# Entry to and exit from six seven-product steps: order lists, VectorE combinations and a further PSUM bank

## The chip, the cores and the metric

The kernel runs on one core of one Trainium2 chip. The metric is device time in microseconds (us) for one execution of the whole program. Three runs of the kernel before took 573.86, 575.05 and 577.16 us; the median is 575.05 us.

The engines are TensorE (PE in the rows; its weight loads are PEld), VectorE (DVE), ScalarE (ACT), GpSimd (POOL) and SyncE (SP, which here only issues DMAs). Each engine takes its instructions strictly in the order in which the program issues them.

## The reference

Attention with rotary embedding, then two feed-forward layers on its 1152 rows of 512 numbers (width inside: 2048). The change touches the first layer and the start of the second.

```python
x = attention(q, k, v)                    # (2, 8, 576, 64) -> (1152, 512)
h = x @ w_in                              # first layer, 512 -> 2048
g = np.where(h > 0, h, np.exp(np.minimum(h, 0)) - 1)
x = g @ w_out                             # 2048 -> 512
h = x @ w2_in                             # second layer
x = (h * np.tanh(np.log1p(np.exp(h)))) @ w2_out
```

## The kernel before, in words

Every matrix product is done as three products of rounded numbers: each operand is split into a high part (ScalarE rounds it) and a remainder (VectorE or GpSimd subtracts it), and high*high, high*low and low*high are added in PSUM. The weights come as 64-bit numbers (512 KB tiles `raw`, three buffers); ScalarE scales their high words (L96), VectorE puts the low bits in (L112, L123), ScalarE rounds (L128), and VectorE or GpSimd makes the remainder (L129).

The first layer has 16 blocks of 128 inner columns. Blocks 0 to 3 are done as six plain units, `units[0]` to `units[5]`: two blocks by a third (384) of the rows each, 24 pairs of matmuls in `g1_mm` (L211). Units 0 to 2 are multiplied in the tail of the attention. The units' way through the activation is `elu` (two ScalarE passes, L256 and L257), `elu_join` (VectorE, L261), `elu_hi` (ScalarE, L266) and `elu_lo` (VectorE, L270). Their product with `w_out` is twelve groups of 12 matmuls (`g2_mm`, L1012), three thirds by four slices; ScalarE copies each group out of PSUM into `Y` (L1041). These groups have two PSUM banks (`ps_h`), the units have two (`ps_s`).

Blocks 4 to 15 are done in pairs, six steps q = 2 to 7, each by a seven-product scheme in the manner of Strassen: `Pair.mm(1)` to `Pair.mm(7)`, here P1 to P7, 12 matmuls each at L1199, over combinations t1 to t4 of the inputs in each half of the rows (`form1`, L1090; their remainders `lo1`, L1094) and sums of the weights (`Pieces.sums`, L907). P1, P6, P7 and P4 add to one bank one after another, P5 and P3 to another, and ScalarE copies the state between them out (L1215); so P6 has to wait for the copy of P1, P7 for that of P6, P4 for that of P7. A step also runs the twelve groups of the step before (H0 to H11, six matmuls each, `g3_mm`, L1029); VectorE adds each into `Y` (L1043). P1, P5, P6 and P2 of a step come ahead of its H0. The order in a step is the hand-written list STEP, which `layer_step` plays.

Entry: `first` plays `unit_step(n)` for each unit, with the combinations of the inputs in between (`first_pieces`; t1 of both halves on GpSimd, the rest on VectorE), then STEP for q = 2, which runs the last four groups of the units when it comes to "or0". Exit: after STEP for q = 7, `seam` runs that step's own twelve groups, splits the new inputs (L1046, L1053) and forms the second layer's combinations (`form`, L975). `second` then does three plain units (`classic`, L211), three output groups (`out_mm`, L1426) and the second layer's steps, beginning with its P1.

The program is played in the order written (a manual schedule), so a list sets the order on all engines.

Of the kernel before, what the change touches and what calls it, by code (L numbers as in the profile page):

```python
# [26 lines left out]
def kernel(  # L27
# [23 lines left out]
    GF = 4  # L51
# [886 lines left out]
    def moe(mp, early):  # L938
# [96 lines left out]
        def g3_y():  # L1035
            if not sums1:
                return
            pair, t, e, o = sums1.pop(0)
            y = Yf[:, e, t * CH:t * CH + CH]
            if pair is None:  # L1040
                nc.scalar.activation(out=y, in_=o, func=AF.Copy)  # L1041
            else:
                nc.vector.tensor_tensor(out=y, in0=y, in1=o, op=ALU.add)  # L1043
            if pair is not None and pair.q == NF // 2 - 1 and e % 2:
                part = (slice(None), slice(e - 1, e + 1), slice(t * CH, t * CH + CH))
                nc.scalar.activation(out=XH[part], in_=Yf[part], func=AF.Copy)  # L1046
                late_xl.append((t, e, part))
            elif late_xl:
                last_xl()

        def last_xl():
            t, e, part = late_xl.pop(0)
            (nc.gpsimd if t and e == 1 else nc.vector).tensor_tensor(  # L1053
                out=XL[part], in0=Yf[part], in1=plain(XH[part]), op=ALU.subtract
            )

        pend, queue1, sums1, late_xl = [], [], [], []
# [38 lines left out]
        def unit_step(n):  # L1096
            m, fp, t = units[n]
            o = early.pop(n) if n in early else g1_mm(m, fp, t)

            def outs(k):  # L1100
                for _ in range(k):
                    if pend:
                        g3_mm()
                        g3_y()

            if n == 2:
                advance(0)
                advance(0)
                prefetch_weights(3)
            if o is not None:  # L1110
                o = elu(units[n], o)
                if n == 5:
                    put_hi(0, "t1")
                    put_hi(1, "t1")
                outs(1)
                o = elu_join(*o)
                if n == 5:
                    lo1(0, "t1", nc.vector)
                    lo1(1, "t1", nc.vector)
                o = elu_hi(*o)  # L1120
                outs(3)
                elu_lo(*o)
            first_pieces(n)
            if n % 2:
                pend.extend((t, e) for e in range(NC))

        ahead[:] = [3, 3]
        w2 = Pieces(0, GF // 2)

        def first_pieces(n):  # L1130
            D, G = nc.vector, nc.gpsimd
            if n == 2:
                w2.load(0)
                w2.load(1)
                for k in range(3):
                    form1(0, "t1", k, G)
                for k in range(3):
                    form1(0, "t3", k, D)
                w2.bits(0, 0, 1, 2)
                w2.bits(1, 0, 1, 2)  # L1140
                for k in range(3):
                    form1(1, "t1", k, G)
                for k in range(2):
# [36 lines left out]
        class Pair:  # L1180
# [96 lines left out]

        STEP = (
# [506 lines left out]
```

## Time and profile before

| what | value |
|---|---|
| runs, median (lowest, highest) | 575.05 us (573.86, 577.16) |
| the profiled execution: its own time | 575.36 us |
| its span in the trace | 573.2 us |
| mean granted TensorE clock | 0.97 of full |
| TensorE matmul busy | 544.3 us, 95% |
| VectorE, ScalarE, GpSimd busy | 436.8 (76%), 342.3 (60%), 221.1 us (39%) |

The time of the profiled execution is 2.2 us more than its span, for what lies around it. A share over the span mixes stages; a stage's own rows say what it waits for. The attention ends near 159 us, the six units and q = 2 lie between 159 and some 230 us, the even steps of 23.7 us run to about 328 us, the last step and the seam to 395 us, and the second layer to the end.

### The profile page before, as it was taken

The numbers are of one execution on the slowest core, as the hardware profiler recorded it, in microseconds if no ns is written. First come the engines' busy times: TensorE is split into PE (matmuls) and PEld (weight loads), VectorE is DVE, ScalarE is ACT, GpSimd is POOL, SyncE is SP. The second block draws the span as 40 slices with busy tenths as digits, with TensorE's granted clock in tenths as the row PEclk, the third lists the DMA queues.
The fourth block names the chain that finished last, engine by engine and source line by source line (L and its number), as shares of the span: only waits on it lengthen the run. The fifth ranks groups of instructions, "written<-read, shape, count | busy, mean of one in ns | idle before, by whom it ended". The sixth has DMA issues, their size and how long they took to land.

```text
span 573.2 us, 9332 instructions
## 1 busy us (share of the span) xinstructions
PE 544.3 (95%) x3436; PEld 490.8 (86%) x3436; DVE 436.8 (76%) x745; ACT 342.3 (60%) x640; POOL 221.1 (39%) x187
## 2 busy tenths in 40 slices
PE   8999999999997986899999996799999999999997
PEld 6778888888996885899999996798899888998986
DVE  6677777778778727878888787788788788878754
ACT  4766767777645426776666765357855546455430
POOL 7999989622293202232222321242012232123200
PEclk9999999999999878799999999699999999999999
DMA  6868889772312022314133142201331422313004
GB/s 207 215 187 223 225 211 245 174 184 86 112 37 75 0 74 73 113 35 148 38 111 112 37 148 74 73 1 38 110 114 40 141 74 74 120 39 100 1 1 165
DMA packets 49405, 60.70 MB, mean 106 GB/s; under 512 B 20944, under 2 KB 38736, under 8 KB 48592
## 3 DMA queue, kind: packets, MB, share of 16 engines
q1 hardware_dynamic: 48816, 59.52, 35.8%
q10 hardware_dynamic: 544, 0.59, 0.3%
q8 instruction: 27, 0.44, 0.3%
q14 instruction: 18, 0.15, 0.1%
HBM read 46.92 MB, written 2.36 MB: 86 GB/s over the span
## 4 chain that ended last, share of the span: by engine, by line
PE 78%; DVE 9%; ACT 4%; DMA 3%; issue 3%; SPq 2%; POOL 1%; ACTq 0%; POOLq 0%
PE ps_s L1199 25%; PE ps_h L1426 17%; PE ps_h L1029 12%; PE ps_s L479 6%; PE psA L599 5%; PE psT L559 4%; PE ps_s L211 3%; PE ps_h L1012 3%; DMA raw<-in_w_in_dram 2%; DVE ta L1090 1%; DMA v_t<-in_vp_dram 1%; SPq L380 1%; DVE gg L975 1%; DVE wv L112 1%; PE psA L668 1%
## 5 line engine op out<-in xcount | busy, mean ns | idle before, releaser
L491 DVE TENSOR_REDUCE mn<-ps_s 128x1 f32<-128x576 f32 x71 | 53.5, 757 | 24.1 <-PE ps_s L479 23.9
L1215 ACT ACTIVATE ta<-ps_s 128x576 f32<-128x576 f32 x58 | 37.5, 647 | 53.9 <-PE ps_s L1199 53.9
L1436 DVE TENSOR_TENSOR Y<-Y,ps_h 128x512 f32<-128x512 f32 (+1 forms) x64 | 43.4, 678 | 26.9 <-PE ps_h L1426 26.6
L513 ACT ACTIVATE P<-ps_s,mn 128x576 f32<-128x576 f32 x71 | 52.4, 739 | 10.6 <-DVE mn L491 9.4
L1043 DVE TENSOR_TENSOR Y<-Y,ps_h 128x384 f32<-128x384 f32 x72 | 39.1, 551 | 17.4 <-PE ps_h L1029 16.4
L1029 PE MATMUL ps_h<-gg,wo0bh 128*128 128x384 f32 x144 | 40.2, 362 | 6.6 <-ACT gg L1249 3.2
L1426 PE MATMUL ps_h<-wo0h,gg 128*128 128x512 f32 x144 | 45.3, 396 | 0.9 <-ACT Y L1434 0.9
L129 POOL TENSOR_TENSOR wo0l<-wu,wo0h 128x512 fp32r<-128x512 f32 x13 | 17.6, 1368 | 73.7 <-ACT wo0h L128 55.1
L1426 PE MATMUL ps_h<-wo0bh,gg 128*128 128x512 f32 (+2 forms) x148 | 45.7, 390 | 0.0
L559 PE MATMUL psT<-idn,P 128*128 128x128 f32 x288 | 42.9, 273 | 0.0
L129 POOL TENSOR_TENSOR wo0bl<-wu,wo0bh 128x512 fp32r<-128x512 f32 x12 | 15.9, 1340 | 64.1 <-ACT wo0bh L128 48.6
L579 ACT ACTIVATE pt<-psT 128x512 f32<-128x512 f32 x40 | 23.8, 594 | 25.7 <-PE psT L559 25.7
L1029 PE MATMUL ps_h<-gg,wo0h 128*128 128x384 f32 x144 | 36.9, 338 | 1.2 <-DVE Y L1043 1.2
L1252 DVE TENSOR_TENSOR gg<-ta,gg 128x576 fp32r<-128x576 f32 x46 | 35.7, 788 | 1.2 <-ACT gg L1249 0.8
L599 PE MATMUL psA<-pt,v_t 128*64 128x256 f32 (+1 forms) x240 | 35.9, 401 | 0.0
L559 PEld LDWEIGHTS psT<-idn,P 128*128 128x128 f32 x288 | 34.7, 141 | 1.3 <-ACT P L508 0.4
L1029 PEld LDWEIGHTS ps_h<-gg,wo0bh 128*128 128x128 f32 x144 | 27.8, 203 | 8.2 <-DVE Y L1043 4.0
L129 POOL TENSOR_TENSOR wi1l<-wv,wi1h 128x512 fp32r<-128x512 f32 x12 | 16.8, 1399 | 43.4 <-ACT wi1h L128 32.9
L1426 PEld LDWEIGHTS ps_h<-wo0bh,gg 128*128 128x128 f32 x148 | 26.9, 188 | 5.5 <-DVE Y L1436 0.2
L1426 PEld LDWEIGHTS ps_h<-wo0h,gg 128*128 128x128 f32 x144 | 26.1, 188 | 6.3 <-ACT Y L1434 1.3
L1249 ACT ACTIVATE gg<-ta 128x576 fp32r<-128x576 f32 x24 | 16.4, 684 | 24.9 <-DVE ta L1244 24.9
L129 POOL TENSOR_TENSOR wi0l<-wv,wi0h 128x512 fp32r<-128x512 f32 x14 | 19.6, 1400 | 24.8 <-ACT wi0h L128 21.1
(254 smaller groups left out, 1727.9 us busy)
## 6 DMA issues: line engine op xcount, KB each, us to landing
raw<-in_w_in_dram SPq DMA_DIRECT2D x32, 512.0 KB, 3.8
raw<-in_w_out_dram SPq DMA_DIRECT2D x32, 512.0 KB, 3.3
qk_t<-in_qk_dram SPq DMA_DIRECT2D x6, 1152.0 KB, 5.6
qa<-qh SPq DMA_DIRECT2D x28, 144.0 KB, 3.2
out_dram<-Y SPq DMA_DIRECT2D x8, 256.0 KB, 2.0
ka<-kh SPq DMA_DIRECT2D x14, 144.0 KB, 4.2
ka<-kl SPq DMA_DIRECT2D x14, 144.0 KB, 3.5
qb<-ql SPq DMA_DIRECT2D x14, 144.0 KB, 3.0
```

What stands on the lines that cost most here:

```text
L129: (by or nc.gpsimd).tensor_tensor(out=lo, in0=u, in1=plain(hi), op=ALU.subtract)
L491: nc.vector.tensor_reduce(out=m[:, 0:1], in_=psS[u][:, :, :HS], axis=AX.XY, op=ALU.min)
L513: nc.scalar.activation(out=P.rearrange("p (j n) -> p j n", j=2), in_=s[:, :, :HS], func=AF.Exp, scale=-1.0, bias=m, accum_out=sm_t[p, g][: ...
L559: nc.tensor.transpose(tv[:, c, :], P[:, k:k + 128], idn)
L599: nc.tensor.matmul(o[64 * h:64 * h + 64, cols], lhsT=v, rhs=rhs, start=(c == 0 and first), stop=(c == 4), skip_group_check=True,)
L1029: nc.tensor.matmul(o, lhsT=w[:, e * 128:e * 128 + 128], rhs=x, start=(k == 0), stop=(k == 5))
L1043: nc.vector.tensor_tensor(out=y, in0=y, in1=o, op=ALU.add)
L1199: nc.tensor.matmul(self.o[r][:, u, :H2], lhsT=w[i][:, cc, :], rhs=XO[u][xn][x][:, cc, :], start=(first and n == 0), stop=(last and n == 3 ...
L1215: nc.scalar.activation(out=self.temp(nm), in_=self.bank(r), func=AF.Copy)
L1252: (by or nc.vector).tensor_tensor(out=self.home(nm, 1), in0=self.temp(nm), in1=plain(self.home(nm, 0)), op=ALU.subtract)
L1426: nc.tensor.matmul(o, lhsT=l, rhs=w[:, es], start=(k == 0), stop=(k == 5))
L1436: nc.vector.tensor_tensor(out=y, in0=y, in1=o, op=ALU.add)
```

## The change: what it does

Three order lists take the place of `unit_step`, `first_pieces`, `seam` and the STEP of the first and the last step. BEGIN holds units 2 to 5 and step q = 2 in one list, LAST holds step q = 7 and the seam in one list; STEP stays for q = 3 to 6 (four entries that called nothing are gone from it). In the lists M is a unit's product, E, J, I, K its activation in the four parts above, H and Y a group and its eviction, f, h, l a combination, its rounding and its remainder, W, Q, S, R the weights of the first (in LAST: of the second layer's first) pair: scale, low bits, sums, rounding; small letters w, p, s, r the same for the next pair; o, or the output weights; c, d, e, x, h, l with m1, u2, u3 or s the activation of the four results of a step; C and D the rounding and remainder of the new inputs.

All combinations and their remainders in the entry are on VectorE. Unit 5 is multiplied into the bank that P5 and P3 use later (`spare_bank`), so units 3, 4 and 5 have three banks.

```diff
-        def unit_step(n):
-            m, fp, t = units[n]
-            o = early.pop(n) if n in early else g1_mm(m, fp, t)
...
-        def first_pieces(n):
-            D, G = nc.vector, nc.gpsimd
...
-                for k in range(3):
-                    form1(0, "t1", k, G)
...
-                for k in range(3):
-                    form1(1, "t1", k, G)
...
+        o2 = [Block(GF + j) for j in range(2)]
+
+        def spare_bank():
+            return g_pool[0].tile([128, 2, 512], F32, tag="s2", name="ps_s2", bufs=1)
...
+        BEGIN = (
+            "v", "W0", "f0t10", "E2", "W1", "J2", "H0", "Y0", "f0t30", "f0t31", "f0t32", "H1",
+            "f0t20", "Q10", "M3", "I2", "H2", "K2", "f0t11", "Y1", "Q00", "Q01", "f0t21", "Y2",
+            "M4", "f0t40", "E3", "f1t30", "f0t12", "H3", "Q11", "h0t1", "J3", "I3", "S3", "f0t41",
+            "M5", "K3", "h0t4", "S1", "l0t1", "S2", "E4", "S4", "J4", "R1", "R2", "I4",
+            "K4", "h0t3", "H4", "h0t2", "Y3", "l0t4", "R0", "E5", "R3", "Y4", "f1t31", "l0t3",
+            "P1", "J5", "f1t32", "h1t3", "f1t20", "I5", "f1t10", "f1t11", "f1t12", "H5", "H6", "Y5",
+            "A0", "h1t1", "A1", "f1t21", "P2", "l0t2", "w0", "l1t1", "Y6", "h1t2", "f1t40", "f1t41",
+            "p00", "K5", "h1t4", "l1t4", "H7", "cm1", "Y7", "l1t2", "dm1", "o00", "l1t3", "P5",
+            "p01", "cm5", "em1", "H8", "P6", "Y8", "o01", "xm1", "cu2", "P3", "du2", "P7",
+            "eu2", "xu2", "cu3", "d22", "hu2", "hm1", "eu3", "w1", "H9", "H10", "lu2", "Y9",
+            "o10", "lm1", "xu3", "P4", "hu3", "lu3", "p10", "p11", "Y10", "s3", "o11", "H11",
+            "r0", "s1", "or0", "cs", "Y11", "or1", "s2", "s4", "es", "r1", "a0", "r2",
+            "r3", "a1",
+        )
...
+        LAST = (
+            "P1", "w0", "cm1", "P5", "o00", "Xs", "o01", "cm5", "p00", "P6", "o10", "P3",
+            "Ks", "cu2", "o11", "or0", "Ls", "H0", "w1", "P2", "or1", "dm1", "P7", "p10",
+            "p11", "H1", "Y0", "p01", "Y1", "H2", "H3", "em1", "H4", "xm1", "r1", "Y2",
+            "du2", "Y3", "H5", "hm1", "a0", "lm1", "cu3", "eu2", "H6", "b0", "H7", "Y4",
+            "xu2", "r0", "P4", "H8", "Y5", "H9", "Y6", "hu2", "lu2", "d22", "Y7", "eu3",
+            "a1", "xu3", "Y8", "cs", "hu3", "H10", "Y9", "Y10", "es", "xs", "lu3", "W0",
+            "Q00", "W1", "H11", "Q01", "Y11", "hs", "Q10", "ls", "b1", "B0", "Q11", "q",
+            "H12", "mish", "H13", "Y12", "Y13", "B1", "S3", "C0", "H14", "S1", "H15", "H16",
+            "Y14", "Y15", "H17", "C1", "Y16", "H18", "D0", "S2", "Y17", "C2", "D2", "Y18",
+            "H19", "Y19", "R0", "S4", "H20", "H21", "D1", "H22", "C3", "Y20", "Y21", "Ft3",
+            "C4", "D3", "Y22", "Gt3", "H23", "Ft2", "Y23", "D4", "Ft4", "Gt2", "C5", "Lt2",
+            "Lt3", "D5",
+        )
...
+            dict(R0="DVE", R1="POOL", R2="DVE", R3="POOL", lm1="DVE", lu2="DVE", lu3="POOL", or0="DVE", or1="DVE", r0="DVE", r1="DVE", r2="DVE", r3="DVE"),
...
+            dict(B0="DVE", D0="POOL", D1="DVE", D2="DVE", D3="DVE", D4="DVE", D5="DVE", Ls="POOL", lm1="POOL", ls="DVE", lu2="POOL", lu3="POOL", or0="DVE", or1="DVE", r0="POOL", r1="DVE", r2="DVE", r3="POOL"),
...
+                elif k == "M":
+                    n = int(r)
+                    at[n] = g1_mm(*units[n], o=spare_bank() if n == 5 else None)
...
+                elif k == "f":
+                    form1(int(r[0]), r[1:3], int(r[3]), nc.vector)
...
+                elif k == "l":
+                    lo1(int(r[0]), r[1:], nc.vector)
...
-        def seam(x, o):
...
+                if q == GF // 2:
+                    layer_step(BEGIN, BY[0], x, None, w, o, on, w2)
...
+                    if q + 1 < NQ:
+                        layer_step(STEP, BY[1], x, prev, w, o, on)
+                    else:
+                        layer_step(LAST, BY[2], x, prev, w, o, on, ahead_pieces)
```

GpSimd in the entry, from the last output weights of the attention's tail to the first remainder of a result `gg`. The kernel before (L1090: t1; L1094: remainders of t2 to t4; L129: weights):

```order
L1090 TENSOR_TENSOR Y<-XH 128x2x288
L1090 TENSOR_TENSOR Y<-Y,XL 128x2x288 x2
L1090 TENSOR_TENSOR Y<-XH 128x2x288
L1090 TENSOR_TENSOR Y<-Y,XL 128x2x288 x2
L129 TENSOR_TENSOR wi1l<-wv,wi1h 128x512
L1094 TENSOR_TENSOR ge<-ta,ge 128x576 x2
L129 TENSOR_TENSOR wi1l<-ws,wi1h 128x512
L1094 TENSOR_TENSOR xt_2324<-ta,xt_2324 128x576
L129 TENSOR_TENSOR wo0l<-wu,wo0h 128x512
L1252 TENSOR_TENSOR gg<-ta,gg 128x2x288
```

The changed kernel, the same stretch of the same engine:

```order
L129 TENSOR_TENSOR wi1l<-wv,wi1h 128x512
L129 TENSOR_TENSOR wi1l<-ws,wi1h 128x256
L1169 TENSOR_TENSOR gg<-ta,gg 128x2x288
```

Six parts of t1 and three remainders have gone from GpSimd to VectorE, and two of the four weight remainders there have changed.

ScalarE in the entry, around the evictions of the second third of the units' groups (L1041). The kernel before; the first row is the high part of unit 3:

```order
L266 ACTIVATE gg<-tc 128x768
L998 ACTIVATE xt_2202<-ta 128x576
L128 ACTIVATE wi1h<-wv 128x512 x2
L998 ACTIVATE ge<-ta 128x576 x2
L256 ACTIVATE tc<-ps_s 128x768
L257 ACTIVATE tc<-tc 128x768
L1041 ACTIVATE Y<-ps_h 128x384
L266 ACTIVATE gg<-tc 128x768
L1041 ACTIVATE Y<-ps_h 128x384 x3
```

The changed kernel, from the fourth eviction (the last of the first third) on; `ps_s_2222` is unit 5 in the further bank:

```order
L1041 ACTIVATE Y<-ps_h 128x384
L128 ACTIVATE wi1h<-wv 128x512
L256 ACTIVATE tc<-ps_s_2222 128x768
L257 ACTIVATE tc<-tc 128x768
L128 ACTIVATE wi1h<-ws 128x256
L1041 ACTIVATE Y<-ps_h 128x384
L998 ACTIVATE xt_2316<-ta 128x576
L266 ACTIVATE gg<-tc 128x768
L1041 ACTIVATE Y<-ps_h 128x384
```

The evictions now stand one by one between the other work, and unit 5's activation comes ahead of the second third's evictions.

VectorE in the exit, around the remainder of the result s of step q = 7 (the remainders of results write `gg`; the join of s is the L1244 row, L1161 in the changed kernel). The kernel before, up to the first additions of that step's own groups:

```order
L112 TENSOR_SCALAR wu_3958<-wu_3958 128x512
L123 SCALAR_TENSOR_TENSOR wu_3958<-raw_3718,wu_3958 128x512
L1252 TENSOR_TENSOR gg_3853<-ta_3865,gg_3853 128x2x288
L1244 SCALAR_TENSOR_TENSOR ta_3949<-sa_3964,ta_3949 128x576
L1252 TENSOR_TENSOR gg_3853<-ta_3949,gg_3853 128x2x288
L112 TENSOR_SCALAR wv_3968<-wv_3968 128x512
L123 SCALAR_TENSOR_TENSOR wv_3968<-raw_3790,wv_3968 128x512
L112 TENSOR_SCALAR wv_3975<-wv_3975 128x512
L123 SCALAR_TENSOR_TENSOR wv_3975<-raw_3876,wv_3975 128x512
L1043 TENSOR_TENSOR Y_2053<-Y_2053,ps_h_3991 128x384
L1043 TENSOR_TENSOR Y_2053<-Y_2053,ps_h_3998 128x384
L1043 TENSOR_TENSOR Y_2053<-Y_2053,ps_h_4009 128x384
```

The changed kernel, from the join of s to the same additions:

```order
L1161 SCALAR_TENSOR_TENSOR ta_3942<-sa_3954,ta_3942 128x576
L112 TENSOR_SCALAR wv_3959<-wv_3959 128x512
L123 SCALAR_TENSOR_TENSOR wv_3959<-raw_3784,wv_3959 128x512
L1043 TENSOR_TENSOR Y_2053<-Y_2053,ps_h_3968 128x384
L112 TENSOR_SCALAR wv_3964<-wv_3964 128x512
L1169 TENSOR_TENSOR gg_3867<-ta_3942,gg_3867 128x2x288
L112 TENSOR_SCALAR wu_3936<-wu_3936 128x512
L123 SCALAR_TENSOR_TENSOR wu_3936<-raw_3718,wu_3936 128x512
L129 TENSOR_TENSOR wo0l_3983<-wu_3869,wo0h_3982 128x512
L123 SCALAR_TENSOR_TENSOR wv_3964<-raw_3871,wv_3964 128x512
L1043 TENSOR_TENSOR Y_2053<-Y_2053,ps_h_3987 128x384
L1043 TENSOR_TENSOR Y_2053<-Y_2053,ps_h_3997 128x384
```

The low bits of the second layer's output weights (`wu`), which stood ahead of the remainders of u3 and s, come behind that of s; the remainders of u2 and u3 have left the engine (they are on GpSimd), and the first layer's last addition and half of the next weights' low bits (`wv`) stand between the join of s and its remainder.

## Rows read from the trace of the kernel before

**Rows 1.** The page's line of the granted TensorE clock, 40 slices

```profile
PEclk9999999999999878799999999699999999999999
```

**Rows 2.** Windows: length, busy us (count) per engine, clock, DMA share, GB/s

```profile
158.90:239.80 80.90, 65.69 (x349) 62.55 (x349) 55.47 (x69) 43.10 (x73) 26.71 (x18) 0.85 0.17 54
242.05:265.77 23.72, 23.72 (x159) 23.72 (x158) 19.34 (x37) 15.59 (x27) 5.78 (x5) 1.00 0.28 79
328.46:395.40 66.94, 58.33 (x320) 55.23 (x320) 55.24 (x81) 37.20 (x58) 17.02 (x13) 0.92 0.20 63
198.20:208.40 10.20, 7.46 (x29) 7.11 (x30) 5.30 (x9) 2.90 (x5) 0.00 (x0) 0.50 0.33 102
358.60:368.70 10.10, 7.82 (x26) 7.32 (x25) 7.45 (x10) 3.31 (x5) 2.90 (x3) 0.50 0.33 104
```

**Rows 3.** The chain that ended last: start, length (us), work

```profile
189.86 4.20 PE ps_s L211 x24
...
209.15 8.49 PE ps_h L1012 x48
...
265.77 3.18 PE ps_s L1199 x24
268.95 6.24 PE ps_h L1029 x36
...
403.33 5.60 PE ps_h L1426 x24
```

**Rows 4.** Waits of TensorE, 158 to 240 us: total, times, longest

```profile
PE ps_s L1199 <- ACT ta L1215: 6.2, 3, 2.7
PE ps_s L1199 <- ACT wi0h L128: 3.9, 1, 3.9
PE ps_h L1012 <- ACT Y L1041: 3.1, 1, 3.1
```

**Rows 5.** Waits of TensorE, 328 to 396 us

```profile
PE ps_h L1029 <- DVE Y L1043: 4.1, 3, 2.3
PE ps_h L1029 <- ACT gg L1249: 3.2, 1, 3.2
```

**Rows 6.** Timeline of ScalarE, entry: start, length (us), instruction

```profile
182.56 0.84 ACT L257 ACTIVATE tc<-tc 128x768 f32<-128x768 f32 x1
183.31 0.47 ACT L1041 ACTIVATE Y<-ps_h 128x384 f32<-128x384 f32 x1
...
224.94 0.68 ACT L1239 ACTIVATE sa<-ta 128x576 f32<-128x576 f32 x1
225.66 0.68 ACT L1240 ACTIVATE sa<-sa 128x576 f32<-128x576 f32 x1
226.25 0.61 ACT L128 ACTIVATE wi0h<-wv 128x512 fp32r<-128x512 f32 x1
```

**Rows 7.** Timeline of VectorE, entry

```profile
164.12 1.98 DVE L1090 TENSOR_TENSOR ta<-XH 128x576 f32<-128x576 f32 x1
...
173.18 0.75 DVE L1090 TENSOR_TENSOR ta<-ta,XH 128x576 f32<-128x576 f32 x1
...
174.64 0.95 DVE L261 SCALAR_TENSOR_TENSOR tc<-tc,ps_s 128x768 f32<-128x768 f32 x1
...
203.30 0.42 DVE L112 TENSOR_SCALAR wv<-wv 128x512 int32<-128x512 int32 x1
203.64 0.68 DVE L123 SCALAR_TENSOR_TENSOR wu<-raw,wu 128x512 int32<-128x512 int32 x1
```

**Rows 8.** Timeline of GpSimd, entry

```profile
161.95 3.52 POOL L1090 TENSOR_TENSOR Y<-Y,XL 128x576 f32<-128x576 f32 x2
165.43 1.95 POOL L1090 TENSOR_TENSOR Y<-XH 128x576 f32<-128x576 f32 x1
```

**Rows 9.** The page's group of additions into Y: busy, mean ns

```profile
L1043 DVE TENSOR_TENSOR Y<-Y,ps_h 128x384 f32<-128x384 f32 x72 | 39.1, 551 | 17.4 <-PE ps_h L1029 16.4
```

**Rows 10.** Loads, 140 to 245 us: count, KB each, us to landing

```profile
raw<-in_w_in_dram SPq DMA_DIRECT2D x7, 512.0 KB, 3.8
```

More of the change, by code (lines that the diff above doesn't have):

```diff
@@ L1043, in g3_y @@
                 nc.vector.tensor_tensor(out=y, in0=y, in1=o, op=ALU.add)
[L1044 to L1057, printed above, removed]
+        pend, queue1, sums1 = [], [], []
         late_pool[0] = mp
@@ L1336, in layer_step @@
                 elif k == "o":
                     o[int(r[0])].bits(2 * int(r[1]))
-                elif k == "r":
-                    w.round(int(r), by(t))
+                elif k == "A":
+                    o[int(r)].load()
                 elif k == "a":
                     on[int(r)].load()
-                    if x.q == NF // 2 - 1:
-                        on[int(r)].bits(0, 1, 2)
+                elif k == "b":
+                    on[int(r)].bits(0, 1, 2)
+                elif k == "B":
+                    on[int(r)].round(eng(t))
+                elif k == "v":
+                    pend.extend((0, e) for e in range(NC))
+                    advance(0)
+                    advance(0)
+                    prefetch_weights(3)
+                elif k == "M":
+                    n = int(r)
+                    at[n] = g1_mm(*units[n], o=spare_bank() if n == 5 else None)
+                elif k == "E":
+                    at[int(r)] = elu(units[int(r)], at[int(r)])
+                elif k == "J":
+                    at[int(r)] = elu_join(*at[int(r)])
+                elif k == "I":
+                    at[int(r)] = elu_hi(*at[int(r)])
+                elif k == "K":
+                    n = int(r)
+                    elu_lo(*at[n])
+                    if n % 2:
+                        pend.extend((n // 2, e) for e in range(NC))
+                elif k == "f":
+                    form1(int(r[0]), r[1:3], int(r[3]), nc.vector)
+                elif k == "h":
+                    put_hi(int(r[0]), r[1:])
+                elif k == "l":
+                    lo1(int(r[0]), r[1:], nc.vector)
+                elif k == "q":
+                    queue1.extend((x, t, e) for t in range(NT // CH) for e in range(NC))
+                elif k == "C":
+                    nc.scalar.activation(out=XH[part(r)], in_=Yf[part(r)], func=AF.Copy)
+                elif k == "D":
+                    eng(t).tensor_tensor(out=XL[part(r)], in0=Yf[part(r)], in1=plain(XH[part(r)]), op=ALU.subtract)
+                elif t == "mish":
+                    warm = mp.tile([128, 1], F32, name="warm")
+                    nc.gpsimd.memset(warm, 0.0)
+                    nc.scalar.activation(out=warm, in_=warm, func=AF.Mish)
+                    mish[0] = True
+                elif k == "F":
+                    form(0, r)
+                elif k == "G":
+                    put_hi(0, r)
+                elif k == "L":
+                    put_lo(0, r)
+                else:
+                    raise ValueError(t)
@@ L1377, in first @@
                 o = on
             return x, o
-        def seam(x, o):
-            w = ahead_pieces
-            w.load(0)
-            x.join("s")
-            x.hi("s")
-            x.lo("s")
-            w.load(1)
-            w.bits(0, 0, 1, 2)
-            for b in o:
-                b.round()
-            w.bits(1, 0, 1, 2)
-            queue1.extend((x, t, e) for t in range(NT // CH) for e in range(NC))
-            for i in range(3 * NC):
-                g3_mm()
-                if i:
-                    g3_y()
-                if i == 1:
-                    warm = mp.tile([128, 1], F32, name="warm")
-                    nc.gpsimd.memset(warm, 0.0)
-                    nc.scalar.activation(out=warm, in_=warm, func=AF.Mish)
-                    mish[0] = True
-                if i in (3, 5):
-                    w.sums(*((0, 1) if i == 3 else (2, 3)))
-                if i == 10:
-                    form(0, "t3")
-                    w.round(0)
-                if i == 11:
-                    form(0, "t2")
-            g3_y()
-            last_xl()
-            form(0, "t4")
-            put_hi(0, "t3")
-            put_hi(0, "t2")
-            put_lo(0, "t3")
-            put_lo(0, "t2")
```

158 lines of the change are left out of this document (46 added, 112 removed), and 14 rows, old and new, of the table STEP.

## Prediction

> **What bounds the kernel now.** I read the page's clock line first, because a busy share of 95% hides where TensorE runs slowly: the slices that fall under full clock lie in two places, 186 to 244 us and 358 to 373 us [rows 1]. These are the entry to and the exit from the seven-product steps, the only places that the change touches. Then the windows [rows 2]. A step in the middle (242.05 to 265.77) keeps TensorE busy for all its 23.72 us at full clock, with VectorE busy 19.3 and ScalarE 15.6 us: such a step can't get shorter, and there is spare time beside it. The entry, from the end of unit 2 (158.9) to the first output group H0 of step q = 3 (239.8), takes 80.9 us with TensorE busy 65.7 at a mean clock of 0.85. The exit, from P1 of q = 7 (328.46) to the second layer's first P1 (395.4), takes 66.9 us with 58.3 busy at 0.92.
>
> Third, the waits of TensorE. In the entry [rows 4] it waits 6.2 us in three stays for ScalarE's copies between P1, P6, P7 and P4, because in STEP the last four groups' evictions stand in front of those copies; 3.9 us for the rounding of the next step's weights; and 3.1 us for an eviction into Y that stands behind both passes of unit 4's activation (it starts at 183.31, right after the pass from 182.56) [rows 6]. In the exit [rows 5] it waits 4.1 us for additions into Y and 3.2 us for the high part of the result s. The waits are paid again in clock: at 198.2 to 208.4 and 358.6 to 368.7, both behind waits, the granted clock was 0.50, that is the 1.2 GHz level, and TensorE was busy 7.5 and 7.8 us there [rows 2]. At full clock that work takes half, so each stretch cost 3.7 to 3.9 us.
>
> **What TensorE must do in any order.** Prices from the chain [rows 3]: a unit 4.20 us; a units' group 8.49 / 4 = 2.12; a product 3.18 / 2 = 1.59; a step's group 6.24 / 6 = 1.04; an output group 5.60 / 4 = 1.40. Entry: three units 12.6, twelve groups 25.5, seven products 11.1, then P1, P5, P6, P2 of q = 3 with 6.4: 55.6 us, so H0 of q = 3 can't come before 158.9 + 55.6 = 214.5. Exit: seven products 11.1, 24 groups 25.0, three units 12.6, three output groups 4.2: 52.9 of the 66.9 us. The most that the change can give is 25.3 + 14.0 = 39.3 us; no matmul is added or removed.
>
> **Entry, part by part.** The evictions stand singly and the four last groups are spread between the products, so each copy comes while a group runs: the 6.2 and 3.1 us have cover. Unit 5 in a further bank lets M5 run before unit 3's and unit 4's banks are read; its price is that P5 must wait until unit 5's join has read that bank, which stands 23 entries and several matmul groups ahead of P5: nothing.
>
> VectorE takes over nine instructions of the combinations from GpSimd, and four in all of q = 2's remainders. From the first part of t1 to the remainder of q = 2's s, which H0 of q = 3 needs, it has 78 instructions: 8 of 768 wide at 0.95 us, 38 of 576 wide at 0.75, 17 of 0.42 (9 shifts, 8 sums), 15 of 0.68 (7 low bits, 8 weight remainders, one of them half as wide) [rows 7]. That is 7.6 + 28.5 + 7.1 + 10.2 = 53.4 us; back to back each hides 0.08 of the one before (203.30 to 203.64 with 0.42), so 47.2 to 53.4 us from 158.9: ready between 206.1 and 212.3, under TensorE's 214.5 if it never waits. It is close, so every wait of VectorE counts in part.
>
> Such waits come from GpSimd: a combination of 0.75 us took 1.98 while GpSimd ran one, which itself took 1.95 against 3.52 / 2 = 1.76 [rows 7, 8]. So the two engines take turns. On GpSimd the six parts of t1 held VectorE off 1.76 us each, on VectorE they cost 0.75: 10.6 against 4.5 us, a gain. The changed entry keeps three instructions on GpSimd (R1, R3, and u3's remainder); each can hold VectorE up to 1.3. I take one such hold on the path, 1.3 us; bounds 0 and 3.9.
>
> Where the Trainium skill speaks against the change: Perfetto Trace Analysis, section Optimizing Scalar/DVE Operations, says that moving work between these two engines might not help, since they share a read port. By that rule the exchange gives nothing: the sum keeps its TensorE terms, and VectorE's 53.4 us, counted with the 6.1 that the exchange saves, come to 59.5 and over the floor by 3.9. The rows above show the sharing (1.98 against 0.75), and also that an instruction on VectorE takes its turn for less than half as long.
>
> What is late next is the hand-over to q = 3. After the last group H11, TensorE has P1 (1.59 us) and then P5, which needs r1, the last but two of the weight roundings. ScalarE has between H11 and r1 an eviction (0.47), a rounding (0.61), both passes of s (0.68 each) and r1 itself (0.61) [rows 6]: 3.05, less overlaps 2.7 to 3.0; P5 waits 1.1 to 1.5, I take 1.4. Behind r1 on ScalarE stands a0, the scaling of a weight tile whose buffer is freed by o11; a load lands in 3.8 us [rows 10], o11 comes some 4 us ahead of a0, so between 0 and 2 us for r2 and P6 behind it; I take 0, since it lies beside the wait for r1. VectorE's arrears of a few us are worked off in q = 3, which leaves it 4.4 us [rows 2].
>
> A wait of TensorE of about a microsecond may or may not bring the lower clock; I put in half of the price of one stretch, 1.9 us (bounds 0 and 3.9). Entry: 214.5 + 1.3 + 1.4 + 1.9 = 219.1 instead of 239.8: -20.7 us.
>
> **Exit, part by part.** VectorE has 81 instructions in 55.2 us there now [rows 2]; the lists move three result remainders and one input remainder to GpSimd and others back, so its work stays near that, under 52.9 only if GpSimd holds it off less than now (13 instructions then, as many now). The high part of s now comes behind a copy (0.61), two passes (1.37), the join (0.75) and two scalings, and its remainder (0.75) behind that: about 5 us after P4, against H8 to H11 (4.2): H12 waits 0.9 instead of 3.2. Behind that remainder VectorE has low bits, a weight remainder and low bits again (2.3 us) before the first addition (0.55 [rows 9]); H14 needs that addition's bank, 2.1 us after H12 starts: another 0.8. The input roundings and remainders come before their units need them; the second layer's combinations lie beside the three units. One hold by GpSimd 1.3 and half a slow stretch 1.9 as above: 52.9 + 0.9 + 0.8 + 1.3 + 1.9 = 57.8 instead of 66.9: -9.1 us.
>
> **Sum.** -20.7 - 9.1 = -29.8 us on the profiled execution's own time of 575.36 us: 545.6. That execution lies 0.3 us from the median of the runs, 575.05, so I take no difference and forecast 546. Two runs of this kernel differ by up to 0.6%, so about 0.5% is what can be told from no change.
>
> **Rivals.**
> - *VectorE becomes the bound.* For it: 53.4 us of work in a stretch whose floor is 55.6, with every activation join in the same queue. If it waits for others as much as in a full step (4.4 of 23.7 us), the entry is 53.4 + 3.9 + 55.6 x 4.4 / 23.7 = 67.6 us and, with TensorE waiting for it, two slow stretches, 7.7: 80.9 - 75.3 = 5.6 gained; the exit with two slow stretches is 63.6, 3.3 gained. Time 566; with only one of the two places so, 551 or 561. Against it: the lists put joins behind work that is ready.
> - *TensorE near its floor*: none of the added waits, 575.4 - 39.3 = 536 to 541. Against it: r1, which follows from the list.
> - *Not faster: the low clock stays.* If TensorE's small waits keep it at 1.2 GHz from unit 5 on, the work behind (eight groups, eleven products: 16.9 + 17.5 = 34.4 us) takes twice as long, +34.4, and undoes the whole entry's and exit's gain: about 575 to 580. It decides from some 30 us at the low level. Against it: in the full steps, where TensorE has work without end, the clock was 1.00, and in the lists it waits less than now, when two such stretches cost 10 us each. The Trainium skill, page TensorE: Matmul & The Clock Gate, section HAM oscillation, describes such loops that wait and go slow again each time; the trace agrees that it happens here, in two stretches of 10 us and no more.
> - *The change doesn't reach the bound*: loads set the time. Against it: no wait of TensorE in either place ends with a load [rows 4, 5]; 572 to 575.
>
> **How the numbers follow.** Forecast (its own range 541 to 552) 0.58; VectorE as the bound, in part or whole (552 to 566) 0.24; near the floor (536 to 541) 0.09; low clock 0.06; loads 0.03. The range 538 to 561 leaves out about 0.2: half of the floor case, the upper part of the second, and the last two. Faster by over 0.5%: 0.92; within 0.5%: 0.03; slower: 0.05.
>
> **What would show it.** Right: H0 of q = 3 near 219, the next full steps at 23.7 us, no six-microsecond wait for copies; P5 of q = 3 waiting for r1; the second layer's P1 some 58 us after P1 of q = 7; clock under 0.9 in no stretch over 10 us. Wrong: VectorE without idle time from 165 to 215 while TensorE waits for combinations or joins; several low stretches in the entry; a load as the releaser of a0 with P6 behind it.

## The result and the profile after

| | before | after |
|---|---|---|
| median of 4 runs | 574.83 us | 545.32 us (545.22 to 545.94) |
| ratio, 95% interval | | 0.9483 [0.9454, 0.9513] |
| profiled execution: time, span | 575.36, 573.2 us | 545.94, 544.1 us |
| mean granted clock | 0.97 | 0.997 |
| entry: unit 2's end to H0 of q = 3 | 80.9 us | 58.4 us |
| exit: P1 of q = 7 to the second layer's P1 | 66.9 us | 61.1 us |

The change is faster by 5.2%. The forecast was 546.0; of its two terms the entry came out 1.8 us better (-22.5 for -20.7) and the exit 3.3 us worse (-5.8 for -9.1), and the attention's end, which the forecast left where it was, came 0.8 us earlier. That the whole lies within 1 us of the forecast is in part luck: these errors cancel.

The page's clock line of the changed kernel, which answers to [rows 1]: one slice under full clock, in the exit, where before there were five.

```profile
PEclk9999999999999999999999998999999999999999
```

The windows of the changed kernel: entry (the row ends 0.16 us behind the first matmul of H0), a middle step, exit; then the exit's first half (seven products, H0 to H11), its twelve last groups (H12 to H23), in these the stretch behind the waits, and the exit's three units; last, VectorE's stretch from the join of s on. Columns as in [rows 2].

```profile
158.10:216.70 58.60, 56.51 (x351) 55.25 (x350) 52.21 (x81) 41.41 (x70) 5.67 (x5) 1.00 0.22 70
242.53:266.25 23.72, 23.72 (x159) 23.72 (x158) 19.19 (x35) 15.58 (x27) 5.25 (x6) 1.00 0.29 88
305.06:366.15 61.09, 56.98 (x320) 52.91 (x320) 51.68 (x81) 37.15 (x59) 17.32 (x12) 0.97 0.22 69
305.06:330.84 25.78, 24.66 (x157) 23.30 (x157) 19.84 (x34) 15.36 (x27) 7.48 (x6) 1.00 0.34 103
330.84:348.98 18.14, 15.35 (x74) 13.79 (x73) 15.29 (x29) 9.16 (x14) 4.82 (x3) 0.91 0.26 88
333.90:337.40 3.50, 3.50 (x11) 3.07 (x12) 3.29 (x7) 0.95 (x3) 1.49 (x1) 0.53 0.70 243
348.98:361.48 12.50, 12.50 (x73) 12.50 (x73) 12.32 (x15) 9.21 (x15) 5.02 (x3) 1.00 0.00 0
330.47:366.15 35.68, 32.69 (x167) 29.98 (x166) 32.21 (x49) 22.16 (x34) 9.93 (x8) 0.95 0.13 45
```

The middle step is what it was, 23.72 us, so all but the 0.8 us of the attention's end was won at the two ends. In the entry's row TensorE is busy 56.5 of 58.6 us at full clock. TensorE's waits in the entry of the changed kernel (total, times, longest), which answer to [rows 4]:

```profile
PE ps_s L1116 <- ACT ta L1132: 0.8, 1, 0.8
PE ps_s L1116 <- ACT wi0h L128: 0.7, 1, 0.7
PE ps_s L1116 <- DVE wi0l L129: 0.4, 1, 0.4
```

Of 6.2, 3.9 and 3.1 us are left 0.8 and 0.7, and 0.4 for a remainder on VectorE, all in the hand-over to q = 3. TensorE's waits in the exit, which answer to [rows 5]:

```profile
PE ps_h L1029 <- DVE Y L1043: 2.0, 4, 0.9
PE ps_h L1029 <- DVE gg L1169: 1.4, 1, 1.4
PE ps_h L1029 <- ACT gg L1166: 0.5, 1, 0.5
PE ps_h L1388 <- ACT Y L1396: 0.2, 1, 0.2
```

Group H12 waits twice for s, 0.5 us for its high part and 1.4 us for its remainder, and behind that TensorE runs at a granted clock of 0.53, the 1.2 GHz level, to 337.4. The other three executions had a mean clock of 1.000 and spans of 543.4 to 543.5 us: this stretch comes in some executions and costs 0.6 to 0.7 us.

### The profile page after: what moved, and what is told of

It reads as the page before. It is cut to its first block, busy times and chain, and to the rows that moved or that the text cites. A ratio compares the mean times of both kernels' runs of the same rounds, so it can differ in the third digit from the quotient of the medians.

```text
span 544.1 us, 9320 instructions
## 1 busy us (share of the span) xinstructions
PE 533.2 (98%) x3436; PEld 480.9 (88%) x3436; DVE 432.2 (79%) x759; ACT 341.7 (63%) x640; POOL 200.7 (37%) x173
## 4 chain that ended last, share of the span: by engine, by line
PE 92%; DVE 4%; ACT 2%; issue 1%; POOL 0%; POOLq 0%; ACTq 0%; DVEq 0%
PE ps_s L1116 25%; PE ps_h L1388 18%; PE ps_h L1029 12%; PE ps_s L479 9%; PE psA L599 8%; PE ps_s L211 6%; PE psT L559 6%; PE ps_h L1012 4%; DVE Y L1043 1%; PE psA L668 1%; PE psL L564 1%; PE psA L533 1%; POOL wo0bl L129 0%; DVE ta L1161 0%; DVE ta L1140 0%
## 5 line engine op out<-in xcount | busy, mean ns | idle before, releaser
L1132 ACT ACTIVATE ta<-ps_s 128x576 f32<-128x576 f32 x58 | 37.5, 646 | 55.5 <-PE ps_s L1116 55.5
L1043 DVE TENSOR_TENSOR Y<-Y,ps_h 128x384 f32<-128x384 f32 x72 | 39.1, 551 | 12.6 <-PE ps_h L1029 11.5
L1029 PE MATMUL ps_h<-gg,wo0bh 128*128 128x384 f32 x144 | 38.7, 350 | 2.8 <-DVE gg L1169 1.4
L129 POOL TENSOR_TENSOR wo0bl<-wu,wo0bh 128x512 fp32r<-128x512 f32 x11 | 15.2, 1392 | 60.2 <-ACT wo0bh L128 53.9
L1169 DVE TENSOR_TENSOR gg<-ta,gg 128x576 fp32r<-128x576 f32 x43 | 31.9, 753 | 0.4
L129 POOL TENSOR_TENSOR wi1l<-wv,wi1h 128x512 fp32r<-128x512 f32 x11 | 15.7, 1428 | 43.9 <-ACT wi1h L128 42.4
L1169 POOL TENSOR_TENSOR gg<-ta,gg 128x576 fp32r<-128x576 f32 x9 | 13.0, 1443 | 51.0 <-ACT gg L1166 35.4
L129 POOL TENSOR_TENSOR wo0l<-wu,wo0h 128x512 fp32r<-128x512 f32 x11 | 14.9, 1363 | 44.9 <-ACT wo0h L128 35.6
L1029 PEld LDWEIGHTS ps_h<-gg,wo0bh 128*128 128x128 f32 x144 | 26.6, 194 | 4.3 <-DVE Y L1043 1.9
L1388 PE MATMUL ps_h<-wo0bl,gg 128*128 128x512 f32 (+2 forms) x74 | 28.9, 391 | 0.0
```

The costliest lines, as they stand in the source:

```text
L129: (by or nc.gpsimd).tensor_tensor(out=lo, in0=u, in1=plain(hi), op=ALU.subtract)
L1029: nc.tensor.matmul(o, lhsT=w[:, e * 128:e * 128 + 128], rhs=x, start=(k == 0), stop=(k == 5))
L1169: (by or nc.vector).tensor_tensor(out=self.home(nm, 1), in0=self.temp(nm), in1=plain(self.home(nm, 0)), op=ALU.subtract)
L1388: nc.tensor.matmul(o, lhsT=l, rhs=w[:, es], start=(k == 0), stop=(k == 5))
```

## The experiments

**Entry and exit apart.** For the entry alone, LAST is filled with the order of STEP and `seam` of the kernel before; for the exit alone, BEGIN is filled with that of `unit_step`, `first_pieces` and STEP. The table of which engine makes which remainder goes back with each, and in the second unit 5 goes back to the ordinary banks. Of each list only the first line is shown.

```diff
         LAST = (
-            "P1", "w0", "cm1", "P5", "o00", "Xs", "o01", "cm5", "p00", "P6", "o10", "P3",
...
+            "P1", "w0", "o00", "cm1", "o01", "P5", "P6", "Xs", "o10", "p00", "Ks", "Ls",
...
```

> BEGIN as in the changed kernel, step q = 7 and the twelve groups behind it in the order of the kernel before. By the prediction's account (terms of the entry alone, -20.7 us) about 554; by the trace of the changed kernel (entry 58.6 us instead of 80.9, attention's end 0.8 earlier) about 552, exit still 66 to 67 us. Rival: entry and exit are not independent (VectorE's arrears run through the steps between them), then this run and the one with LAST alone do not add up to the whole, by more than 2 us.

```diff
         BEGIN = (
-            "v", "W0", "f0t10", "E2", "W1", "J2", "H0", "Y0", "f0t30", "f0t31", "f0t32", "H1",
...
+            "v", "E2", "H0", "Y0", "J2", "I2", "H1", "Y1", "H2", "Y2", "H3", "Y3",
...
-                    at[n] = g1_mm(*units[n], o=spare_bank() if n == 5 else None)
+                    at[n] = g1_mm(*units[n])
...
```

> Entry in the order of the kernel before, LAST as in the changed kernel. By the prediction's account (-9.1 us) about 566; by the trace of the changed kernel (exit 61.1 us instead of 66.9) about 569. Rival: the exit's gain came out small because the changed entry sends something on; then this run shows an exit under 59 us.

Measured: 550.56 us for the entry alone, ratio 0.9585 [0.956, 0.9609], and 569.03 for the exit alone, 0.9899 [0.9867, 0.993], against 574.17 before. That is -23.6 and -5.1, together -28.7 where the whole change gives -29.5: the two places add up, and the exit's gain is small by itself. From P1 of q = 7 to the second layer's P1 it takes 66.0 us in the first version and 62.8 in the second.

**Is it VectorE in place of GpSimd?** First the six parts of t1 back on GpSimd, in the same order: the six entries become "g", which runs the same combination on GpSimd. Two of the changed lines:

```diff
-            "P1", "J5", "f1t32", "h1t3", "f1t20", "I5", "f1t10", "f1t11", "f1t12", "H5", "H6", "Y5",
+            "P1", "J5", "f1t32", "h1t3", "f1t20", "I5", "g1t10", "g1t11", "g1t12", "H5", "H6", "Y5",
...
+                elif k == "g":
+                    form1(int(r[0]), r[1:3], int(r[3]), nc.gpsimd)
```

> The six parts of t1 go back to GpSimd, all else stays. By taking turns (1.76 us of hold against 0.75 us of work each, 6.1 us in all, of which VectorE has about 2.5 us in hand before P5 and P6 want its remainders, and under 2 us of idle time before that): 1 to 4 us slower than the changed kernel, 546.5 to 549, with TensorE waiting at P5 or P6 of q = 2. Rival, the rule that moving work between the two engines gives nothing: 545.3 within 0.5. A second rival: two engines work side by side, then it is as fast or faster.

Measured: 545.41 us, ratio 0.9501 [0.9472, 0.953]: no loss. The entry's window, and three combinations on VectorE beside three on GpSimd:

```profile
158.10:216.70 58.60, 56.62 (x353) 55.68 (x353) 53.94 (x75) 41.08 (x71) 15.10 (x11) 1.00 0.22 70
...
182.41 1.86 DVE L1078 TENSOR_TENSOR ta<-ta,XL 128x576 f32<-128x576 f32 x1
184.30 1.88 DVE L1078 TENSOR_TENSOR ta<-ta,XH 128x576 f32<-128x576 f32 x1
186.21 1.87 DVE L1078 TENSOR_TENSOR ta<-ta,XL 128x576 f32<-128x576 f32 x1
...
182.22 1.43 POOL L1078 TENSOR_TENSOR Y<-XH 128x576 f32<-128x576 f32 x1
183.73 3.73 POOL L1078 TENSOR_TENSOR Y<-Y,XL 128x576 f32<-128x576 f32 x2
```

The two engines take turns as the prediction read it (1.86 to 1.88 for 0.75), and VectorE is busy 1.7 us longer with six instructions fewer; the prediction's 6.1 us for the exchange were too many, since it took 1.76 us of hold for each part and a held instruction here takes 1.1 longer. But TensorE's waits are the same three as above, so even the 1.7 us are not waited for. The rule of the Trainium skill (Perfetto Trace Analysis, Optimizing Scalar/DVE Operations) that offloading between these two might not help agrees with the time here.

Second, more work on VectorE:

```diff
-            "f0t32", "H1",
-            "f0t20", "Q10", "M3",
+            "f0t32", "f0t10", "H1",
+            "f0t20", "Q10", "f0t10", "M3",
...
```

In the lines left out, "f1t10" is put in behind "J3", "S1", "J4" and "J5".

> Six more instructions on VectorE in the entry: the first step of t1 is computed again (two times in the first half, four times in the second, before it is used; the result is the same), 6 x 0.67 to 0.75 = 4.0 to 4.5 us. If TensorE is the bound and VectorE has 2.4 to 2.6 us in hand at P5 and P6 (as the trace of the changed kernel has it), 0.6 to 1.6 us slower: 546 to 547. If VectorE is the bound: 4 us or more, 549.5 or later. If there is ample room: 545.3.

Measured: 545.47 us, ratio 0.9527 [0.947, 0.9585]; three executions lay between 545.28 and 545.52, one at 551.11, for which I have no cause. The entry window:

```profile
158.10:216.70 58.60, 56.52 (x349) 54.94 (x348) 55.13 (x87) 40.98 (x70) 5.42 (x5) 1.00 0.21 69
```

VectorE did 2.9 us more and the end of the entry did not move: it has more room than the 2.4 us that I read off two remainders. In the changed kernel it waits 2.0 us for TensorE and 1.5 for ScalarE between 195 and 201 us; here the first of these waits is gone and the second is as long as before, so the arrears are worked off there.

**The further bank.**

```diff
-                    at[n] = g1_mm(*units[n], o=spare_bank() if n == 5 else None)
+                    at[n] = g1_mm(*units[n])
```

> Unit 5 goes into one of the two ordinary banks of the units, all else stays. The prediction costs the further bank at nothing and counts on no gain from it alone: unit 3's join is done at 172.1, unit 5 starts after 174; P2 at 187.1, long after unit 5's join at 182.7: 545.3 within 0.5. Rival: the further bank carries part of the gain, because units 3 and 4 are read late; then unit 5 or P1 or P2 waits for a join, 1 to 4 us slower.

Measured: 545.93 us (545.0 to 546.83), ratio 0.9505 [0.9479, 0.9531]; TensorE waits nowhere between 158 and 200 us. The bank is worth nothing that can be told.

**Spreading the last four groups.**

```diff
-            "H8", "P6", "Y8", "o01", "xm1", "cu2", "P3",
+            "P6", "H8", "Y8", "H9", "Y9", "H10", "Y10", "H11", "Y11", "o01", "xm1", "cu2", "P3",
... (H9 to H11 and Y9 to Y11 are gone from their places behind)
```

> In the entry the last four groups H8 to H11 and their evictions stand together behind P6, ahead of the copies for P7 and P4, as STEP had them for q = 2; all else stays. If spreading them is what gives the copies cover (the prediction's first term): the copies come up to three groups (6.4 us) later, and with them u2, u3, s and the hand-over: 3 to 8 us slower than the changed kernel, 548 to 553, part of it in low clock. Rival: the gain of the entry comes from the other moves (evictions of the second third, early roundings of the weights): 545 to 546.5.

Measured: 552.61 us, ratio 0.9649 [0.9605, 0.9693], 7.3 us slower than the changed kernel. TensorE's waits in the entry:

```profile
PE ps_s L1116 <- ACT wi0h L128: 3.0, 1, 3.0
PE ps_s L1116 <- ACT ta L1132: 2.0, 2, 1.3
PE ps_s L1116 <- DVE wi0l L129: 1.8, 1, 1.8
```

H0 of q = 3 starts 5.8 us later than in the changed kernel (222.3 for 216.5), so the order of these groups carries 6 to 7 of the entry's 23 us. Less of it than I thought are the copies (2.0); more is the hand-over, where P1 of q = 3 now waits 3.0 and 1.8 us for its weights: no group is left to cover u3, s and the roundings.

**The hand-over.** One move, and then a larger one:

```diff
-            "cs", "Y11", "or1", "s2", "s4", "es", "r1", "a0", "r2",
+            "cs", "Y11", "or1", "s2", "s4", "r1", "es", "a0", "r2",
```

> In the entry the rounding r1 stands ahead of the two passes of s on ScalarE (1.37 us). P5 of q = 3 waits 0.7 us for r1, which then comes 1.3 us earlier: 544.6 (0.5 to 0.8 faster). Rival: the remainder of the same weights on VectorE, or the copy that P6 waits for, takes its place: 545.3 within 0.3.

```diff
-            "r0", "s1", "or0", "cs", "Y11", "or1", "s2", "s4", "es", "r1", "a0", "r2", "r3", "a1",
+            "r0", "s1", "cs", "Y11", "s2", "s4", "r1", "es", "r2", "or0", "a0", "r3", "or1", "a1",
```

> At the end of the entry the roundings and remainders of the output weights (or0, or1), which only H0 of q = 3 needs, stand behind r2 and r3, and r1 stands ahead of the passes of s. VectorE is busy 16.2 of 17.0 us there, so if its queue is what TensorE waits for (r1's remainder took the place of r1 when that alone was moved), 1.28 us of it taken out of the way give 1.0 to 1.5: 544.0. Rival: H0 or P6 then waits for what was put back: 545.3 within 0.4.

Measured: 547.18 us for the first, ratio 0.9528 [0.9504, 0.9552], and 552.47 for the second, 0.9616 [0.9591, 0.9641]; both are slower. Of the first one's 1.9 us its profiled execution shows 0.3 in the entry; its mean clock was 0.994 to 0.997 in all six executions. In the profiled one the low stretch lies behind H12's waits in the exit, as in the changed kernel (334.5 to 338.2 us at 0.54); why all six had a low clock is not settled. With r1 ahead TensorE waits 1.1 us for r1's remainder on VectorE (1.5 in all) and 1.1 for the copy: the rival. In the second version P5 does not wait any more, but P6 waits 5.0 us for its copy, and the granted clock is 0.50 from 214 to 220 us, the 1.2 GHz level. ScalarE in that version; L96 are the scalings a0, a1 and w0, L1132 the copy:

```profile
210.57 0.62 ACT L128 ACTIVATE wo0h<-wu 128x512 fp32r<-128x512 f32 x1
212.03 0.66 ACT L96 ACTIVATE wu<-raw 128x512 f32<-128x512 f32 x1 [0.84 <-DVE wo0l L129]
212.59 0.40 ACT L128 ACTIVATE wi0h<-ws 128x256 fp32r<-128x256 f32 x1
212.90 0.61 ACT L128 ACTIVATE wo0h<-wu 128x512 fp32r<-128x512 f32 x1
214.27 0.67 ACT L96 ACTIVATE wu<-raw 128x512 f32<-128x512 f32 x1 [0.76 <-DVE wo0l L129]
214.84 0.66 ACT L96 ACTIVATE wv<-raw 128x512 f32<-128x512 f32 x1
215.39 0.65 ACT L1132 ACTIVATE ta<-ps_s 128x576 f32<-128x576 f32 x1
```

There are two buffers `wu`: a0 and a1 may not write before or0's and or1's remainders have read. Moved late, they stop ScalarE twice, and the copy behind them is 2.8 us later than in the changed kernel (215.39 for 212.60).

**The exit.** The remainder of u2 goes to VectorE:

```diff
-            lu2="POOL", lu3="POOL", or0="DVE",
+            lu2="DVE", lu3="POOL", or0="DVE",
-            "hu2", "lu2", "d22", "Y7", "eu3", "a1", "xu3",
+            "hu2", "d22", "Y7", "eu3", "a1", "lu2", "xu3",
```

> The remainder of u2 in the exit goes from GpSimd to VectorE, into VectorE's idle time ahead of the join of u3 (1.07 us). If GpSimd's hold of the sum of u3 (1.95 us for 0.75) is what makes u3, s and so H12 late: about 1.2 us earlier at each, 544.1 (0.8 to 1.5 faster). Rival: the exit is long because VectorE's own work is, or for the waits of H12 by themselves: 545.3 within 0.4, or slower by the 0.7 us of added work.

Measured: 545.09 us (544.47 to 545.98), ratio 0.949 [0.9468, 0.9513]: 0.2 us, not to be told from none. In the changed kernel GpSimd holds the sum of u3 (first the remainder u2 on GpSimd, then the sum on VectorE); in this version it does not:

```profile
323.81 1.42 POOL L1169 TENSOR_TENSOR gg<-ta,gg 128x576 fp32r<-128x576 f32 x1
...
323.89 1.95 DVE L1140 TENSOR_TENSOR ta<-ta 128x576 f32<-128x576 f32 x1
```

```profile
324.79 0.75 DVE L1140 TENSOR_TENSOR ta<-ta 128x576 f32<-128x576 f32 x1
```

From P1 to H12 it takes 25.1 us instead of 25.8, but from H12 to the second layer 35.1 where it was 35.3: what comes before H12 is worth 0.7, and H12 waits as before (0.4 and 1.5). Next, s's remainder ahead of the low bits:

```diff
-            "lu3", "W0", "Q00", "W1", "H11", "Q01", "Y11", "hs", "Q10", "ls", "b1",
+            "lu3", "W0", "W1", "H11", "Y11", "hs", "ls", "Q00", "Q01", "Q10", "b1",
```

> In the exit the low bits of the next input weights (three instructions, 1.5 us on VectorE) stand behind the remainder of s and no longer ahead of it. H12's second matmul waits for that remainder from 332.5 to 333.9; ScalarE has the high part ready at 332.0, so it can come 1.0 us earlier: 544.3 (0.7 to 1.1 faster; 1.5 more in an execution that had the low clock behind this wait). Rival: the low bits are then late for the additions into Y and the weights behind them, and the wait moves to H14 or to the second layer: 545.3 within 0.4.

Measured: 548.02 us, ratio 0.9532 [0.9507, 0.9557], slower by 2.7: H12's second wait fell from 1.4 to 0.4 us, and a wait of 2.4 us for an addition came behind it. The rival holds in kind, though it put the price at nothing. Then both (`lu2` on VectorE again), with the copy of s ahead of the scalings and the low bits between and behind the first additions:

```diff
-            "eu3", "a1", "xu3", "Y8", "cs", "hu3", "H10", "Y9", "Y10", "es", "xs", "lu3", "W0",
+            "eu3", "lu2", "xu3", "cs", "Y8", "hu3", "H10", "Y9", "Y10", "es", "xs", "lu3", "a1",
-            "Q00", "W1", "H11", "Q01", "Y11", "hs", "Q10", "ls", "b1", "B0", "Q11", "q", "H12", "mish", "H13", "Y12", "Y13", "B1",
+            "H11", "Y11", "hs", "W0", "ls", "W1", "q", "H12", "Q00", "Q01", "mish", "H13", "Y12", "Q10", "Y13", "Q11", "b1", "B0", "B1",
... (lu2="DVE" as above)
```

> In the exit the remainder of u2 goes to VectorE; the copy of s and its two passes stand ahead of the scalings of the next weights on ScalarE; and the low bits and output-weight roundings stand behind the remainder of s, spread between the first additions into Y and not in one block ahead of them. If H12's wait (2.6 us lost in that group) comes from s's own chain behind u3 and the scalings: 1.5 to 2.5 faster, 543.3. Rival: VectorE is full in the exit's second half (11.3 of 14.0 us, then 11.7 of 12.0), and what is put back returns there as waits for additions: 545.3 within 0.5, or slower.

Measured: 546.62 us (545.63 to 547.57), ratio 0.9521 [0.9496, 0.9547]. H12's waits are 0.46 and 0.44 us, and TensorE waits 3.0 us for Y14, which stands behind 4 us of other work on VectorE (1.0 of it a hold by GpSimd: a sum of 0.42 us took 1.43). Last, that work spread singly, from Y12 on:

```diff
...
+            "Y12", "Q01", "H14", "Y13", "C0", "Q10", "H15", "Y14", "D0", "Q11", "H16", "Y15", "C1", "b1",
+            "H17", "Y16", "B0", "H18", "Y17", "C2", "S3", "S1", "H19", "Y18", "D2", "S2", "H20", "Y19",
```

> As the run before (the remainder of u2 on VectorE, s's copy and passes ahead of the scalings), but low bits, sums and the output weights' remainder stand singly between the additions Y12 to Y19, one to an addition, where they stood in a block of 3.9 us between Y13 and Y14 that kept TensorE waiting 3.0 us. VectorE's work is the same. If the order on VectorE is what the exit loses its time by: H12 waits under 1 us, no addition is waited for longer than 1 us, 542.5 to 544. Rival: the amount of VectorE's work bounds the exit's second half; then the waits only change places, 545.3 within 0.5 or slower.

Measured: 545.4 us (544.97 to 545.58), ratio 0.9497 [0.9473, 0.9522]: the time of the changed kernel. H12 waits under 1 us as expected (0.5 and 0.4), but two additions are waited for 1.3 and 1.4 us, so the waits have changed places. The stretch from the start of H12 to the second layer's P1 in this version:

```profile
330.30:365.61 35.31, 30.80 (x164) 28.05 (x164) 34.22 (x48) 22.41 (x34) 9.03 (x6) 1.00 0.14 45
```

VectorE is busy 34.2 of 35.3 us, TensorE 30.8 at full clock. But some 5.5 of the 34.2 us are holds by GpSimd, in six instructions, where the changed kernel has 2.4 in its stretch from the join of s on. Both long waits for an addition come behind one: a shift of 0.42 us that took 1.62 (at 336.58) and a sum of 0.42 that took 1.50:

```profile
339.44 0.62 PE L1029 MATMUL ps_h<-gg,wo0bh 128*128 128x384 f32 x2 [1.31 <-DVE Y L1043]
...
344.52 0.62 PE L1029 MATMUL ps_h<-gg,wo0bh 128*128 128x384 f32 x2 [1.43 <-DVE Y L1043]
...
342.50 1.50 DVE L907 TENSOR_TENSOR ws<-wv 128x256 f32<-128x256 f32 x1
```

So VectorE with the holds in its queue bounds this version; its own work, some 28.7 us, is less than TensorE's, and whether that work alone would bound the exit is not shown. The second layer's units start 1.2 us earlier than in the changed kernel (347.80 for 348.98) and its P1 0.5 us (365.61 for 366.15); the span is 543.6 us, no shorter than the 543.4 to 543.5 of the changed kernel's other executions. No version of the exit that I ran beats the changed kernel by more than can be told.

## Why the prediction was right, and where its steps were wrong

- **TensorE's floor and the middle step: right.** The exit's three units take 12.5 us (348.98 to 361.48), for 12.6.
- **Copies, evictions and early roundings: right** that they get cover; 13.2 us of waits in [rows 4] became 1.9, and the low stretches of the entry went with them. There were three of these and not one: the prediction prices 198.2 to 208.4 us and says "two stretches of 10 us and no more" for the entry and the exit together, but the kernel before has two more in the entry:

```profile
184.40:187.80 3.40, 3.40 (x13) 3.40 (x12) 2.46 (x4) 1.55 (x3) 1.08 (x1) 0.53 0.02 5
225.80:235.60 9.80, 5.79 (x23) 5.09 (x22) 8.66 (x10) 8.45 (x15) 3.86 (x3) 0.50 0.00 1
```

  The sum does not suffer, since it is built up from TensorE's work and not from what is taken away. Which move gave how much is settled for the last four groups alone (6 to 7 us); the other 16 us were not taken apart.
- **VectorE close behind, "every wait of VectorE counts in part": wrong.** 1.7 us of longer work with t1 on GpSimd, and six more instructions, cost no time, so putting t1 on VectorE is no part of the gain that can be told. The term of 1.3 us for a hold in the entry came to 0.4 at most: a sum of 0.42 us took 1.48 (at 205.48), and r0's remainder behind it is what P1 of q = 3 waits for.
- **The hand-over: right for P5, wrong for P6.** P5 starts 1.5 us later than the 1.59 us of P1 allow (1.4 predicted): TensorE waits 0.4 us for r0's remainder and 0.7 for r1, and the rest goes with starting again. P6 comes another 1.5 us late, where the prediction took 0 "since it lies beside the wait for r1": its copy stands behind a0, r2, r3, a1 and w0 on ScalarE, which works from r1 (209.55) to the copy (212.60) without a pause. Together the entry is 2.8 us over its floor of 55.6, where 4.6 were predicted. Moving r1 alone brought its remainder as the next wait.
- **Low clock in the entry, 1.9 us: none came.** Waits of 0.4 to 0.8 us did not lower it here. The Trainium skill's loop of waits and slow stretches (TensorE: Matmul & The Clock Gate, HAM oscillation) does not occur in the changed kernel; its trace has one stretch, in the exit.
- **Further bank and loads at nothing: right** (545.93 with two banks; no wait of TensorE ends with a load).
- **The exit: the step that failed is to compare sums over the whole of it, TensorE's floor of 52.9 us with VectorE's 55.2 "near that", and to add two short waits for VectorE's queue.** VectorE's work is not spread evenly. In H0 to H11 it is busy 19.8 of 25.8 us; from the join of s on it is busy 32.2 of 35.7 us, where TensorE needs 12 x 1.04 + 12.6 + 4.2 = 29.3. Most of the time (5.6 of 8.2 us over the floor) is lost in H12 to H23: there VectorE is busy 15.3 us, TensorE's work is 12.5, and it takes 18.1. The waits are H12's two for s and one of 0.9 us for an addition; the low stretch and starting again make up the rest. In the three units behind, TensorE runs its 12.5 us without a wait and VectorE is busy for 12.3 of them, so what is put off from H12 to H23 finds little room there. About 2.4 us of the 32.2 is GpSimd's hold, in three instructions that lie in these units (0.75 us each when not held); in the changed kernel they keep TensorE from nothing. They and the weight remainders beside them:

```profile
356.76 1.62 DVE L1002 TENSOR_TENSOR xt<-gg,xt 128x576 fp32r<-128x576 f32 x1
358.31 3.06 DVE L975 TENSOR_TENSOR gg<-Y 128x576 f32<-128x576 f32 x2
...
355.66 2.11 POOL L129 TENSOR_TENSOR wi0l<-ws,wi0h 128x512 fp32r<-128x512 f32 x1 [10.58 <-ACT wi0h L128]
357.73 1.80 POOL L129 TENSOR_TENSOR wi0l<-wv,wi0h 128x512 fp32r<-128x512 f32 x1
```

  So two engines with nearly 30 us of work each stand in one stretch, and neither has room for the other's waits. Each rearrangement of the exit moved the waits and left the time. In the terms: H0 to H11 cost 2.2 us over their 23.6 (for the hold of 1.3), H12 to H23 5.6 over 12.5 (0.9 + 0.8 + 1.9 predicted), the outputs 0.5. H12's wait alone was 1.9 us for the 0.9. That VectorE's order and amount of work cause the loss is read from these rows; no run took work off VectorE there.
- **s's remainder "about 5 us after P4": it was 7.8** (P4's matmuls end at 325.97, the remainder at 333.76). Counted were copy, passes, join and scalings; left out were the passes of u3 and a scaling ahead of the copy on ScalarE (it starts at 327.81), and three instructions of low bits and an addition ahead of the remainder on VectorE. But shortening this chain alone, as three runs did, gave at most 0.7 us before H12 and nothing at the end.

The rival "VectorE becomes the bound" is thus refuted for the entry (67.6 us forecast by it) and lies nearer the measured exit than the sum does (63.6 forecast, 61.1 measured, 57.8 in the sum), though by luck in part: it counts two low stretches, 7.7 us, and one short one came.

Open: whether the exit gets shorter with GpSimd's five weight remainders taken out of the stretch behind H12; that was not tried. The 5.5 us of holds in the last version are the reason to try it.

## What to carry to other kernels

Compare the engines' work in stretches that end where the dependences end, not over a whole stage: over the whole exit VectorE's 52 us and TensorE's 53 look even, but cut at s VectorE is busy 20 of 26 us and then 32 of 36. Before making an off-path engine faster, ask what waits for it; here its slack took 2.9 us of added work without a trace. When a wait is removed by moving an instruction, list what shares its queue and its buffers: r1's rounding gave way to its remainder, and or0 moved late stopped ScalarE through the buffer it was to free.

## What was not expected of the hardware

GpSimd holds VectorE's small integer work too, and by more in proportion. In the last version a shift of 0.42 us took 1.62 beside a remainder on GpSimd (first row), while the addition just ahead of it, which reads PSUM, took its usual 0.55 beside the same remainder:

```profile
335.55 2.37 POOL L1324 TENSOR_TENSOR XL<-Y,XH 128x768 fp32r<-128x768 f32 x1 [6.15 <-ACT XH L1322]
...
336.12 0.55 DVE L1043 TENSOR_TENSOR Y<-Y,ps_h 128x384 f32<-128x384 f32 x1
...
336.58 1.62 DVE L112 TENSOR_SCALAR wu<-wu 128x512 int32<-128x512 int32 x1
```
